# Attention over channels and a gelu MLP on one core: v of block 2 turned on TensorE, the last chunk's steps in order of landing, the first loads in halves

## The chip, the cores and the metric

The kernel runs on 1 core of one Trainium2 chip. The time is what the device takes for one execution, in microseconds (us); runs of the kernel before and of the changed kernel are taken on the same chip and compared. A profiled execution gives the trace: each instruction with its engine, its start and its length, and each DMA with its issue and landing. The engines are TensorE (PE; its weight loads are shown apart as PEld), VectorE (DVE), ScalarE (ACT), GpSimd (POOL) and the sync engine (SP), which here only issues DMAs.

## What is computed

```python
def _attn_ref(q, k, v, tau):                      # q, k, v: 4 x 6080 x 256, tau = 1
    qn = q / (np.linalg.norm(q, axis=1, keepdims=True) + 1e-06)
    kn = k / (np.linalg.norm(k, axis=1, keepdims=True) + 1e-06)
    s = kn.transpose(0, 2, 1) @ qn / tau          # 256 x 256 for each batch
    s = s - s.max(-1, keepdims=True)
    a = np.exp(s)
    a /= a.sum(-1, keepdims=True) + 1e-09
    return (v @ a).astype(np.float32)

def _moe_ref(x, w_in, w_out):                     # x: 24320 x 256
    h = x @ w_in                                  # w_in: 256 x 2048
    c = np.float32(np.sqrt(2.0 / np.pi))
    g = 0.5 * h * (1.0 + np.tanh(c * (h + 0.044715 * h * h * h)))
    return (g @ w_out).astype(np.float32)         # w_out: 2048 x 256
```

The second function is applied to the result of the first. Inputs and output are float32.

## The kernel before

**Stages.** For each batch the kernel needs G = q^T k over all 6080 rows and the sums of squares of the columns of q and k. From these it makes eT, the exponentials of the scaled scores, and then AW = a @ w_in, a 256 x 2048 matrix, so that h = v @ AW needs no separate product with a. For batch 0 this must be done before anything else can start; for batches 1 to 3 it is done a little at a time among the work of the batch before.

**Start (batch 0).** q and k come in six chunks, numbered 0 to 5, of 8, 7, 8, 8, 8 and 8 rows per partition. Chunk 0 is loaded as float32 by two DMAs, q on SP's queue and k on ACT's (`load_first`, L113), and cast on ScalarE (q) and VectorE (k), each in two halves of four rows (`cast_first`, L122 and L124). The other chunks are loaded by POOL with a cast to bf16 on the way (L99); the last one, chunk 5, in five pieces (`PIECES`, `load_last`, L141): q rows 0-3, k rows 0-4, k rows 5-7, q rows 4-5, q rows 6-7. POOL has eight semaphores for its DMAs, so the ninth issue waits until the first has landed, and so on. For each chunk there are squares (q on ScalarE L192/L202, k on VectorE L194/L204), the products G (`gram_row`, L247, two for each row), and the sums of squares as products with ones (`ss_rows`: q by L268, k by L274). `warm(n)` (L369) issues n products whose result nobody reads.

Behind chunk 5 POOL loads the first 512 rows of v (`load_v0(0)`, L314, cast to bf16), w_in in five pieces (L886), half of w_out, v of block 1, the other half of w_out (L647), and v of block 2 by `cast_v`, a cast into DRAM. TensorE runs `warm(8)`, turns v of block 0 (`pe_vt`, L324, eight transposes of 128 x 128 into PSUM), VectorE copies the result into vT (`pe_vt_copy`, L330), and `scores` (L294 to L306) and `first_aw` (L345 to L363) make eT, the row sums, their reciprocals rs and the first columns of AW.

**Blocks.** Then come 48 blocks n = 0 to 47, twelve for each batch, of 512 rows of v (448 in the last of a batch). For each: v transposed into vT (blocks 0 and 1 on TensorE, all others by `cast_v` on POOL, L152, and a transposing DMA on SP, `load_vt`, L162); 2048 columns of h in eight pairs of 256 (`mm1`, L520), except that some sets of two pairs are made by a seven-product scheme (`small`, L596, with sums on VectorE L558 to L561 and L617/L620); gelu on ScalarE (L530, L622, L627, L630) into g; and g @ w_out by the same seven-product scheme on halves (`product`, L725, with seven prepared weights `wcomb`, and sums T1 to T4 on VectorE, L686 to L702). The result is turned on VectorE (L750) and stored by SP (L815).

**The order.** Each engine works through its instructions in program order, and the program order is written out by hand: `WINDOW[n]` names one of the strings in `ORDER` for block n, and its words are issued one after the other, for all engines alike. A word ends in +k or -k when it belongs to block n + k or n - k. The words that matter here: g0 to g7 are pairs of h, G0 to G7 their gelus; awP and acP a part of AW of batch 0 and its copy; T1a, T2a, T2b and so on the sums; M1A to M7B the products with w_out, a half each; p... the preparation of w_out (pA11, pF0, pS1, pF1, pS2, pS4, pS3 on VectorE, L657 to L675; pA12 and pNA on ScalarE, L671 and L673); vs the sums of vT; cq, y5, ap, ax copies and sums of the product's parts; rowI a row of G for the next batch; lq, lk, lv, lt the loads of q, k and v and the transposing load; vtp the turning of v of block 1 on TensorE, vtc0 and vtc1 its copies.

**Buffers.** h uses two buffers of two PSUM banks, so a pair of h waits for the gelu two pairs earlier. Turned v of block 1 uses PSUM tag `s`, as parts of AW do. `load_v0` and the results share the three buffers of the pool `yout`; the two halves of w_out share the two buffers of the squares.

Of the kernel before, what the change touches and what calls it, by code (L numbers as in the profile page):

```python
# [18 lines left out]
def kernel(  # L19
# [10 lines left out]
    nc = tc.nc  # L30
# [75 lines left out]
    def load_first():  # L106


        r0, n = chunks_of(0)[0]
        assert not with_rest(0, 0)  # L110
        st = gp.tile([128, 2, n, 256], FP32, tag="g", name="qk_f32")
        for which, eng in ((0, nc.sync), (1, nc.scalar)):
            eng.dma_start(out=st[:, which], in_=(q, k)[which][0, 0 : R * 128, :].rearrange(  # L113
                "(p r) c -> p r c", r=R)[:, r0 : r0 + n, :])
        return st
# [704 lines left out]
    with tc.manual_schedule():  # L820
# [24 lines left out]
        WARM = [0, 4, 8, 8, 10, 6]  # L845
# [20 lines left out]
        warm(WARM[c])  # L866
        square_rows(c, 0, 0, 4, "act")
        ss_rows(c, 0, range(0, 4))
        square_rows(c, 1, 0, 5, "dve")
        for i in range(4):  # L870
            gram_row(0, c, i)
        ss_rows(c, 1, range(0, 5))
        square_rows(c, 1, 5, 8, "dve")
        square_rows(c, 0, 4, 6, "dve")
        for i in (4, 5):
            gram_row(0, c, i)
        ss_rows(c, 1, range(5, 8))
# [10 lines left out]
        load_v0(1)  # L888
        load_wout(1)
        cast_v(2)  # L890
# [24 lines left out]
        def step(what, n):  # L915
# [28 lines left out]
            elif what[:3] == "vtc":  # L944
                pe_vt_copy(1, int(what[3]))
            elif what[0] == "p":
                prep_wout(what)
            elif what == "lt":
                load_vt(n)
            elif what == "lv":  # L950
                cast_v(n, GATE[0])
            elif what in ("lq", "lk"):
                load_one(b, c, "qk".index(what[1]), GATE[0])
            else:
                mm2_step(n, what)
# [17 lines left out]
    24, 25, 26, 15, 16, 17, 18, 19, 20, 27, 28, 29, 30, 31, 32, 33, 34, 35, 36, 36, 37,  # L973
    38, 39, 40,
]
ORDER = [
    """g0 lt+2 lv+3 aw3 G0 aw2 ac3 g1 ac2 aw5 G1 aw4 lq+1 ac5 g2 SW0 g3 G2 ac4 aw7 G3 aw6 ac7 g4
    ac6 g5 T1a G4 lk+1 vtp G5 g6 vtc0 pA11 g7 G6 vtc1 T2a M1A G7""",
    """g0 pF0-1 lt+2 lv+3 M1B-1 G0 g1 pS1-1 pF1-1 G1 M5A-1 M5B-1 cq-1 g2 pS2-1 lq+1 T2b-1 g3 G2
    pS4-1 M6A-1 G3 M6B-1 g4 pS3-1 y5-1 g5 G4 ap-1 T1a M3A-1 G5 w0m1+1 M3B-1 lk+1 T3b-1 g6  # L980
    pA12-1 vs+1 g7 G6 c12-1 T3a-1 M7B-1 G7 M2B-1 T4a-1 M2A-1 T4b-1 pNA-1 M7A-1 w0m5+1 ax-1""",
    """g0 w0cq T3b-1 lt+2 w0y5 lv+3 row1-1 c11a-2 M4A-2 G0 T2b-1 w0m6 M5B-1 w0ap row3-1 ksq-1
    M4B-2 T2a-1 w0m2 w0m7 row0-1 w0ax w0m3 g3 w0Gq c21-2 lq+1 T3a-1 M5A-1 G3 M1B-1 T4a-1 M1A-1
    c22-2 w0Gx g4 SW1-2 y5-1 cq-1 g5 c11-2 G4 lt+3 lv+4 vs+1 w0m4 M6B-1 w0Gr M6A-1 qsq-1 g6
    ap-1 T1a lk+1 M3A-1 G6 row2-1 M3B-1 f1-1 w0m1+1 G5 M7A-1 T4b-1 w0m5+1 M7B-1 w0y5+1 c12-1
    row5-1 row3 ax-1 w0cq+1 row2 T2a row4-1 g7 ksq f2-1 w0m6+1 row0 w0ap+1 M4B-1 G7 M2A-1
    M2B-1 qsq M4A-1 c11a-1""",
    """g0 f3-2 c21-2 w0m7 G0 w0m2 T2b-1 w0m3 M5A-1 w0ax M1A-1 w0Gq T3a-1 g3 vs+1 w0Gx M1B-1 G3
    w0m4 f1-1 lq+1 M5B-1 g4 cq-1 c22-2 w0Gr w1m5 T1a G4 M6B-1 M6A-1 lt+3 lv+4 w1m1 y5-1 row1-1
    f2-1 w1cq g7 ap-1 w1y5 T4b-1 w1m6 G7 row5-1 w1ap M3A-1 lk+1 row4-1 T3b-1 M3B-1 qsq w0m5+1  # L990
    c12-1 w1m7 w1m2 w1ax w1m3 M7B-1 w1Gq T4a-1 M2A-1 w1m4 c11-2 M2B-1 w1Gr T2a M7A-1 w0y5+1
    row0 ax-1 w0m1+1 w1Gx""",
    """g0 c11a-2 w0cq T3b-1 M4A-2 G0 T3a-1 row5-1 w0m6 M4B-2 f3-2 ksq-1 row2-1 w0ap g3 c21-2
    T2b-1 w0m3 G3 w0m7 w0m2 w0ax M5B-1 lq+1 M1A-1 w0Gq T4a-1 M1B-1 f4-2 w0m4 cq-1 M5A-1 w0Gr
    f1-1 w1m5 M6A-1 y5-1 w1m1 M6B-1 f2-1 w1cq lt+3 lv+4 g4 ap-1 w1y5 c22-2 w0Gx w1m6 c11-2
    M3B-1 w1ap G4 M7B-1 vs+1 row3-1 M3A-1 qsq lk+1 w1m7 f3-1 g7 w1ax T4b-1 w1m3 G7 row4-1 w1m2
    c12-1 w1m4 row1-1 f4-1 M7A-1 w1Gr row2 w1Gq ax-1 M2A-1 T1a w0m1+1 w0m5+1 M2B-1 w0y5+1""",
    """g0 T2a-1 w0cq w1Gx-1 M4A-2 c11a-2 T4a-1 w0m6 G0 M4B-2 w0ap M5A-1 ksq-1 M5B-1 c22-2 c21-2
    row1-1 w0m2 vs+1 w0m7 w0m3 g3 w0Gq w0ax lq+1 T2b-1 M1B-1 G3 w0m4 c11-2 M1A-1 T3a-1 g4 w0Gr
    f1-1 cq-1 w1m5 G4 row4-1 M6A-1 lt+3 lv+4 T4b-1 w1m1 M6B-1 f2-1 y5-1 w1cq g7 ap-1 w1y5  # L1000
    T3b-1 w1m6 G7 M3A-1 w1ap lk+1 M3B-1 M7B-1 w0Gx c12-1 w1m7 ksq M7A-1 w1ax w1m3 w0m5+1 ax-1
    w1m2 w1m4 T1a M2A-1 w1Gr M2B-1 w1Gq row4 c11a-1 row3-1 w0m1+1 f3-1 row0-1 w0cq+1 M4B-1
    c11-1 M4A-1 w0y5+1 row5-1 qsq c21-1 w0m6+1""",
    """g0 w0ap f4-2 M5A-1 w1Gx-1 w0m3 c22-2 w0m7 G0 w0m2 w0ax row2-1 M1A-1 w0Gq T3a-1 M1B-1 w0m4
    T2a-1 g3 cq-1 T3b-1 w0Gr lq+1 M5B-1 G3 f1-1 g4 T2b-1 row0-1 G4 w1m1 M6A-1 T4a-1 w1m5 f2-1
    M6B-1 lt+3 lv+4 y5-1 w1cq g7 ap-1 w1y5 f3-1 w1m6 w0Gx row1-1 w1ap M3B-1 G7 M3A-1 vs+1 lk+1
    w1m7 w1m2 ksq row5-1 w1ax M7B-1 M7A-1 c12-1 T1a w1m3 w1m4 M2A-1 w1Gr M2B-1 ax-1 w1Gq
    w0m5+1 T4b-1 row3-1 w0m1+1 row1 c11a-1 w0cq+1 row0""",
    """g0 T2a-1 w0y5 c11-2 w1Gx-1 w0m6 M4B-2 w0ap G0 M4A-2 f4-2 row4-1 w0m3 qsq-1 w0m7 c22-2 g3
    w0ax w0m2 c21-2 G3 M5A-1 T2b-1 lq+1 w0m4 M1A-1 f1-1 w0Gr row3-1 M1B-1 w0Gq T4a-1 row5-1  # L1010
    w1m1 w1m5 T4b-1 cq-1 M5B-1 w1cq g4 f2-1 lt+3 lv+4 w1y5 T3a-1 w1m6 y5-1 M6A-1 G4 w1ap
    row2-1 M6B-1 f3-1 w0Gx w1m2 T3b-1 w1m3 w1m7 qsq lk+1 g7 ap-1 w1ax M7A-1 f4-1 G7 M3B-1 vs+1
    w1m4 M3A-1 w1Gr M7B-1 c12-1 w1Gq row1 ax-1 w0m5+1 w0m1+1 T1a M2A-1 w0cq+1 M2B-1 w1Gx""",
    """g0 c22-2 w0y5 c11a-2 row2-1 T3a-1 G0 w0m6 M4B-2 w0ap M5B-1 ksq-1 T2b-1 M4A-2 w0m7 c21-2 g3
    w0ax M1A-1 f1-1 G3 w0m2 w0m4 M1B-1 T2a-1 w0Gr w0m3 M5A-1 f2-1 cq-1 T3b-1 row4-1 w0Gq w1m5
    w1m1 c11-2 M6B-1 T4b-1 y5-1 M6A-1 w0Gx lt+3 lv+4 g4 ap-1 w1cq T4a-1 w1y5 M3A-1 f3-1 G4
    w1m6 M3B-1 w1ap row3-1 M7A-1 qsq c12-1 w1m3 vs+1 M7B-1 g7 ax-1 ksq T1a row4 row0 w1m7
    M4A-1 w1ax M2A-1 G7 f4-1 M2B-1 w1m4 c11a-1 row5-1 w1Gr w1m2 f1 M4B-1 w1Gq row1 row2 row0-1
    f2 row5 w0m5+1 f3 w0m1+1 T3a""",
    """lq+4 g0 w0cq c21-2 w0y5 M5B-1 T2a-1 G0 w0m6 M1A-1 w0ap M1B-1 w1Gx-1 f4-1 row3-1 w0m7 cq-1  # L1020
    g3 T2b-1 gc w0ax w0m3 G3 w0m2 M5A-1 T4a-1 w0m4 ss c11-2 w0Gr T3b-1 w0Gq w1m5 sv M6A-1
    T4b-1 pow w1m1 y5-1 M6B-1 c22-2 w1cq g4 lt+3 lv+4 ap-1 w1y5 vs+1 w1m6 G4 M7A-1 w1ap lk+4
    M7B-1 kf M3A-1 w0Gx ax-1 g7 kr T1a w1m7 G7 M3B-1 w1m3 c12-1 w1m2 krp w1ax w1Gq M4A-1 S1+1
    w0m5+1 w1m4 S0+1 w1Gx M2A-1 T2a w1Gr M2B-1 T3a w0y5+1 M4B-1 w0m1+1 th0+1 c21-1""",
# [197 lines left out]
```

## Time and profile before

| | us |
|---|---|
| median of 4 runs | 697.99 (697.83 to 698.2) |
| the profiled execution's own time | 698.2 |
| its span, first to last instruction | 696.4 |
| TensorE busy in the span | 675.4 |
| first product of h | 38.48 |
| TensorE idle before 38.48 | 13.68 |
| TensorE idle from 38.48 to 680 | 0.63 |
| TensorE idle in the last 16.4 us | 6.64 |

The idle times are the lengths of the stretches less TensorE's busy time in them (0.00, 8.89, 7.73 and 8.18 us busy in the stretches from 0, 10, 20 and 30 on). The mean granted clock of TensorE is 0.998. The two loads of chunk 0 landed 8.4 and 8.6 us after their issue at 0.74. A line of the timeline gives start, length, engine, line, operation, tiles and how often; "idle before <-releaser" is how long the engine stood and what ended it.

### The profile page before, as it was taken

How to read it: one execution, taken by the hardware profiler on the slowest of the kernel's cores; microseconds unless marked ns; L12 is line 12 of the kernel's file. 1: busy time of each engine (PE TensorE's matmuls, PEld its weight loads, DVE VectorE, ACT ScalarE, POOL GpSimd, SP SyncE). 2: the span in 40 equal slices, each digit the busy share in tenths (PEclk: the TensorE clock that was granted, in tenths of full speed). 3: DMA queues.
4: the chain of work that ended last, by engine and by line, in shares of the span. 5: the costliest groups of instructions: out<-in, count | busy, mean ns of one | idle time of the engine just before them, and what ended most of it. 6: DMA issues, size and time to landing. Idle time of an engine off the chain costs nothing.

```text
span 696.4 us, 14406 instructions
## 1 busy us (share of the span) xinstructions
PE 675.4 (97%) x5499; PEld 530.5 (76%) x5499; DVE 630.0 (90%) x1243; ACT 616.7 (89%) x894; POOL 73.1 (11%) x135
## 2 busy tenths in 40 slices
PE   3899999999999999999999999999999999999996
PEld 2756778777777777777777777777777888888785
DVE  4489899999998889999999889999999999999996
ACT  5279999998889999998888999999888999999993
POOL 4321100111001001101010010010000000000000
PEclk9999999999999999999999999999999999999999
DMA  9999886775787976747577787683564464453315
GB/s 242 207 262 136 141 150 123 124 107 98 118 129 116 131 128 109 114 81 126 86 131 126 118 126 125 96 138 56 79 101 67 77 103 74 71 99 59 59 34 88
DMA packets 161733, 79.33 MB, mean 114 GB/s; under 512 B 149472, under 2 KB 152672, under 8 KB 160672
## 3 DMA queue, kind: packets, MB, share of 16 engines
q0 software_dynamic: 13952, 39.72, 34.8%
q1 hardware_dynamic: 146608, 37.41, 32.0%
q10 hardware_dynamic: 1104, 1.28, 0.6%
q8 instruction: 43, 0.70, 0.4%
q14 instruction: 26, 0.21, 0.1%
HBM read 78.91 MB, written 36.83 MB: 166 GB/s over the span
## 4 chain that ended last, share of the span: by engine, by line
PE 93%; DMA 4%; DVE 1%; issue 0%; ACT 0%; POOL 0%; DVEq 0%; ACTq 0%; POOLq 0%
PE r L725 23%; PE h L520 22%; PE p L725 17%; PE rb L596 13%; PE qp L596 9%; PE G L247 5%; DMA t<-in_k_dram 2%; PE awp L460 2%; DMA t<-in_q_dram 1%; PE ss L281 0%; DVE xw L620 0%; PE ss L274 0%; PE warm L369 0%; PE rk L405 0%; DVE t L686 0%
## 5 line engine op out<-in xcount | busy, mean ns | idle before, releaser
L725 PEld LDWEIGHTS <-wcomb 128*128 128x128 bf16 x2688 | 262.4, 98 | 42.7 <-issue 0.2
L530 ACT ACTIVATE g<-h 128x1024 bf16<-128x1024 f32 (+1 forms) x178 | 179.7, 1014 | 16.2 <-PE h L520 14.8
L725 PE MATMUL r<-t,wcomb 128*128 128x256 bf16 (+1 forms) x1152 | 164.7, 271 | 0.1
L520 PE MATMUL h<-vT,aw 128*128 128x512 bf16 (+1 forms) x648 | 164.6, 377 | 0.1
L622 ACT ACTIVATE g<-qp 128x1024 bf16<-128x1024 f32 (+1 forms) x103 | 104.6, 1015 | 5.8 <-PE qp L596 3.9
L725 PE MATMUL p<-g,wcomb 128*128 128x256 bf16 (+1 forms) x760 | 106.7, 271 | 0.0
L520 PEld LDWEIGHTS <-aw 128*128 128x128 bf16 x712 | 69.4, 98 | 49.0 <-issue 0.7
L596 PEld LDWEIGHTS <-sw 128*128 128x128 bf16 x824 | 80.2, 98 | 27.5 <-issue 0.9
L192 ACT ACTIVATE sq<-t 128x1536 bf16<-128x1536 bf16 (+4 forms) x59 | 79.3, 1359 | 7.3 <-DMA t<-in_q_dram 7.3
L617 DVE TENSOR_TENSOR qp<-rb,yw 128x512 f32<-128x512 f32 (+1 forms) x103 | 71.0, 689 | 12.7 <-PE rb L596 8.8
L596 PE MATMUL rb<-tv,sw 128*128 128x256 bf16 (+1 forms) x412 | 78.0, 271 | 0.2 <-DVE qp L617 0.2
L620 DVE TENSOR_TENSOR xw<-rb,yw 128x512 f32<-128x512 f32 (+1 forms) x103 | 69.5, 675 | 4.9 <-PE rb L596 4.1
L596 PEld LDWEIGHTS <-aw 128*128 128x128 bf16 x618 | 60.4, 98 | 13.0 <-issue 1.4
L612 ACT ACTIVATE qp<-rb 128x512 f32<-128x512 f32 (+1 forms) x103 | 59.7, 580 | 10.4 <-PE rb L596 5.8
L630 ACT ACTIVATE g<-xw 128x512 bf16<-128x512 f32 (+1 forms) x103 | 63.3, 625 | 1.6 <-DVE xw L620 1.5
L615 ACT ACTIVATE yw<-qp 128x512 f32<-128x512 f32 (+1 forms) x103 | 61.2, 594 | 3.9 <-PE qp L596 2.1
L627 ACT ACTIVATE g<-rb 128x512 bf16<-128x512 f32 (+1 forms) x103 | 61.1, 596 | 3.8 <-PE rb L596 2.6
L698 DVE TENSOR_TENSOR t<-g,t 128x1024 bf16<-128x1024 bf16 (+1 forms) x96 | 63.6, 667 | 0.6
L700 DVE TENSOR_TENSOR t<-g 128x1024 bf16<-128x1024 bf16 (+1 forms) x96 | 63.8, 672 | 0.0
L702 DVE TENSOR_TENSOR t<-t,g 128x1024 bf16<-128x1024 bf16 (+1 forms) x96 | 63.5, 669 | 0.0
L247 PE MATMUL G<-t 128*128 128x256 bf16 (+1 forms) x352 | 58.1, 273 | 1.6 <-DMA t<-in_k_dram 1.6
L686 DVE TENSOR_TENSOR t<-g 128x2048 bf16<-128x2048 bf16 (+1 forms) x48 | 57.4, 1196 | 0.1
(131 smaller groups left out, 879.6 us busy)
## 6 DMA issues: line engine op xcount, KB each, us to landing
out_dram<-ot SPq DMA_DIRECT2D x174, 128.0 KB, 3.0
vb<-in_v_dram POOLq DMA_DIRECT2D x42, 256.0 KB, 4.6
t<-in_q_dram POOLq DMA_DIRECT2D x21, 384.0 KB, 5.1
t<-in_k_dram POOLq DMA_DIRECT2D x21, 384.0 KB, 6.2
wst<-in_moe_w_out_dram POOLq DMA_DIRECT2D x2, 1024.0 KB, 10.4
t<-in_q_dram POOLq DMA_DIRECT2D x3, 512.0 KB, 15.1
t<-in_k_dram POOLq DMA_DIRECT2D x3, 512.0 KB, 17.0
out_dram<-ot SPq DMA_DIRECT2D x12, 112.0 KB, 2.6
```

The lines of the kernel that those rows point to most:

```text
L192: nc.scalar.activation(o, t[:np_, r, :], AF.Square)
L247: nc.tensor.matmul(G[b][:, jc, :], lhsT=qt[:np_, r, jc * 128 : jc * 128 + 128], rhs=kt[:np_, r, :], start=first and jc == 0, stop=jc == 1, ...
L520: mm = nc.tensor.matmul(hp[:, u, :cols], lhsT=AW[b][:, cc, fc * 128 : fc * 128 + 128], rhs=vt_tiles[n][:, cc, :cols], start=cc == 0, stop= ...
L530: nc.scalar.activation(gs(n)[:, 2 * p : 2 * p + 2, :cols], HP.pop((n, p))[:, :, :cols], AF.Gelu_apprx_tanh)
L596: GATE[0] = nc.tensor.matmul(acc[:, u * hc : u * hc + hc], lhsT=lhs[:, u * 128 : u * 128 + 128], rhs=rhs, start=m in (1, 5) and u == 0, st ...
L617: nc.vector.tensor_add(qp(n, i)[:, 1, :c], RB[n, i][:, :c], YW[n, i][:, :c])
L620: nc.vector.tensor_add(XW[n, i][:, :c], RB[n, i][:, :c], YW.pop((n, i))[:, :c])
L622: nc.scalar.activation(gs(n)[:, 2 * pa : 2 * pa + 2, :c].rearrange("p u (t x) -> p t u x", t=2), QP.pop((n, i))[:, :, :c].rearrange("p t ( ...
L698: nc.vector.tensor_sub(o, quarter(n, 1, 1, f0, f1), ts[1][:, f0:f1, :hc])
L700: nc.vector.tensor_sub(o, quarter(n, 1, 1, f0, f1), quarter(n, 0, 1, f0, f1))
L702: nc.vector.tensor_sub(o, ts[2][:, f0:f1, :hc], quarter(n, 1, 0, f0, f1))
L725: nc.tensor.matmul(ACCS[n, acc][:, :hc], lhsT=wcomb[:, w, fc, :], rhs=x, start=first and k == 0, stop=k == 3, skip_group_check=True)
```

## The change

- `load_first` issues four DMAs instead of two: rows 0 to 3 of q on SP and of k on ACT, then rows 4 to 7 on the same queues.
- The six dummy products ahead of chunk 5 are left out. In chunk 5, the sums of squares of q rows 0-3 go behind the first four rows of G, and those of k rows 5-7 ahead of the next two rows of G.
- v of block 2 is loaded by `load_v0(2)`, between v of block 1 and the second half of w_out, instead of `cast_v(2)` behind it. It is turned on TensorE (new word vtq, at the end of block 0) and copied on VectorE (vtr0 and vtr1, at the start of block 1). The transposing load of block 2 (lt+2 in block 0) is gone.
- `ORDER` has new strings for blocks 0 to 16, and `WINDOW` has been renumbered. Apart from the words just named, all words are there as often as before, in another order and partly in another block. From block 17 on the order on TensorE is the same as before; in blocks 18, 21, 25 and 30 loads move by a place or two.

```diff
--- before.py
+++ after.py
@@ -109,9 +109,10 @@
         r0, n = chunks_of(0)[0]
         assert not with_rest(0, 0)
         st = gp.tile([128, 2, n, 256], FP32, tag="g", name="qk_f32")
-        for which, eng in ((0, nc.sync), (1, nc.scalar)):
-            eng.dma_start(out=st[:, which], in_=(q, k)[which][0, 0 : R * 128, :].rearrange(
-                "(p r) c -> p r c", r=R)[:, r0 : r0 + n, :])
+        for h in range(2):
+            for which, eng in ((0, nc.sync), (1, nc.scalar)):
+                eng.dma_start(out=st[:, which, h * 4 : h * 4 + 4], in_=(q, k)[which][0, 0 : R * 128, :].rearrange(
+                    "(p r) c -> p r c", r=R)[:, r0 + h * 4 : r0 + h * 4 + 4, :])
         return st
 
     def cast_first(st):
@@ -842,7 +843,7 @@
         win_bf = const.tile([128, 2, D], BF16)
         wcomb = const.tile([128, 7, 8, 128], BF16)
         nch = len(chunks_of(0))
-        WARM = [0, 4, 8, 8, 10, 6]
+        WARM = [0, 4, 8, 8, 10]
         for c in range(nch - 1):
             if c == 0:
                 cast_first(first)
@@ -863,18 +864,17 @@
         c = nch - 1
         ss_rows(c - 1, 1)
         ss_rows(c - 1, 0)
-        warm(WARM[c])
         square_rows(c, 0, 0, 4, "act")
-        ss_rows(c, 0, range(0, 4))
         square_rows(c, 1, 0, 5, "dve")
         for i in range(4):
             gram_row(0, c, i)
+        ss_rows(c, 0, range(0, 4))
         ss_rows(c, 1, range(0, 5))
         square_rows(c, 1, 5, 8, "dve")
         square_rows(c, 0, 4, 6, "dve")
+        ss_rows(c, 1, range(5, 8))
         for i in (4, 5):
             gram_row(0, c, i)
-        ss_rows(c, 1, range(5, 8))
         ss_rows(c, 0, range(4, 6))
         square_rows(c, 0, 6, 8, "dve")
         for i in (6, 7):
@@ -886,8 +886,8 @@
             nc.gpsimd.dma_start(out=win_bf[:, :, f0:f1], in_=wi[:, :, f0:f1])
         load_wout(0)
         load_v0(1)
+        load_v0(2)
         load_wout(1)
-        cast_v(2)
         warm(8)
         pe_vt(0, "r")
         scores(0)
@@ -943,6 +943,10 @@
                 pe_vt(1, "s")
             elif what[:3] == "vtc":
                 pe_vt_copy(1, int(what[3]))
+            elif what == "vtq":
+                pe_vt(2, "s")
+            elif what[:3] == "vtr":
+                pe_vt_copy(2, int(what[3]))
             elif what[0] == "p":
                 prep_wout(what)
             elif what == "lt":
@@ -970,94 +974,95 @@
 
 WINDOW = [
     0, 1, 2, 3, 4, 5, 6, 7, 8, 9, 10, 11, 12, 13, 14, 15, 16, 17, 18, 19, 20, 21, 22, 23,
-    24, 25, 26, 15, 16, 17, 18, 19, 20, 27, 28, 29, 30, 31, 32, 33, 34, 35, 36, 36, 37,
-    38, 39, 40,
+    24, 25, 26, 27, 28, 17, 18, 19, 20, 29, 30, 31, 32, 33, 34, 35, 36, 37, 38, 38, 39,
+    40, 41, 42,
 ]
 ORDER = [
-    """g0 lt+2 lv+3 aw3 G0 aw2 ac3 g1 ac2 aw5 G1 aw4 lq+1 ac5 g2 SW0 g3 G2 ac4 aw7 G3 aw6 ac7 g4
-    ac6 g5 T1a G4 lk+1 vtp G5 g6 vtc0 pA11 g7 G6 vtc1 T2a M1A G7""",
-    """g0 pF0-1 lt+2 lv+3 M1B-1 G0 g1 pS1-1 pF1-1 G1 M5A-1 M5B-1 cq-1 g2 pS2-1 lq+1 T2b-1 g3 G2
-    pS4-1 M6A-1 G3 M6B-1 g4 pS3-1 y5-1 g5 G4 ap-1 T1a M3A-1 G5 w0m1+1 M3B-1 lk+1 T3b-1 g6
-    pA12-1 vs+1 g7 G6 c12-1 T3a-1 M7B-1 G7 M2B-1 T4a-1 M2A-1 T4b-1 pNA-1 M7A-1 w0m5+1 ax-1""",
...
+    """g0 lv+3 aw3 G0 aw2 g1 ac2 ac3 aw4 G1 aw5 lq+1 ac4 g2 ac5 g3 G2 aw6 G3 g4 ac6 SW0 aw7 G4 g5
+    lk+1 ac7 vtp G5 pA11 g6 vtc0 g7 vtc1 G6 T1a vtq G7""",
+    """g0 vtr0-1 vtr1-1 lt+2 lv+3 g1 T2a-1 G0 T2b-1 M1B-1 G1 pF0-1 g2 g3 G2 pS1-1 w0m1+1 pF1-1
+    lq+1 M1A-1 G3 g4 cq-1 pS2-1 pNA-1 g5 pS4-1 M6B-1 G5 M5A-1 pS3-1 M6A-1 G4 M5B-1 g7 vs+1
+    y5-1 g6 ap-1 G7 T3a-1 lk+1 M3A-1 T3b-1 pA12-1 M7A-1 T4b-1 w0m5+1 M7B-1 w0cq+1 row0 ax-1
+    row1 w0y5+1 M3B-1 T4a-1 G6 w0m6+1 M4B-1 c12-1 w0ap+1 M4A-1 qsq M2A-1 c21-1 M2B-1 row2
+    c11a-1 M1B ksq T1a w0m2+1 w0m7+1 w0m3+1""",
...
```

## The prediction

> **What bounds the kernel now.** I read the page first, then the busy time by stretches, then the chain of waits, then the first 75 us of the timeline with the time that each DMA took to land. The page says that TensorE is nearly all of the chain:
>
> ```profile
> span 696.4 us, 14406 instructions
> ...
> PE 675.4 (97%) x5499; PEld 530.5 (76%) x5499; DVE 630.0 (90%) x1243; ACT 616.7 (89%) x894; POOL 73.1 (11%) x135
> ...
> PE 93%; DMA 4%; DVE 1%; issue 0%; ACT 0%; POOL 0%; DVEq 0%; ACTq 0%; POOLq 0%
> ```
>
> The stretches (columns: stretch, length, busy time and count of each engine, granted clock, DMA share, GB/s) show where TensorE is not full:
>
> ```profile
> 20.00:30.00 10.00, 7.73 (x81) 6.42 (x79) 4.20 (x4) 3.85 (x3) 2.71 (x4) 1.00 1.07 211
> 30.00:38.48 8.48, 8.18 (x105) 6.86 (x103) 4.43 (x11) 3.82 (x9) 5.22 (x7) 1.00 1.29 201
> 38.48:60.00 21.52, 21.52 (x127) 12.04 (x128) 19.95 (x34) 18.04 (x20) 3.31 (x6) 1.00 1.11 232
> 60.00:140.00 80.00, 80.00 (x637) 62.15 (x636) 73.14 (x144) 76.77 (x103) 10.05 (x19) 1.00 0.82 134
> 140.00:200.00 60.00, 59.76 (x474) 45.68 (x473) 57.51 (x118) 53.40 (x83) 7.28 (x12) 1.00 0.68 108
> 200.00:680.00 480.00, 479.61 (x3921) 381.91 (x3919) 451.08 (x899) 446.54 (x666) 34.80 (x65) 1.00 0.61 98
> ```
>
> From 38.48, the first h product, to 680 TensorE idles 0.24 + 0.39 = 0.63 us. So the time is: when h starts, plus the TensorE work behind it, plus those idle tenths, plus a drain that is not touched. Before 38.48 the DMA engines are full (share 1.07) and TensorE is not. The chain of waits tells what sets 38.48 (columns: start, length, what):
>
> ```profile
> 11.28 17.40 DMA t<-in_k_dram
> 28.68 0.04 issue
> 28.72 1.91 PE G L247 x16
> ...
> 31.88 0.68 PE warm L369 x6
> ...
> 35.56 0.90 PE warm L369 x8
> 36.45 0.46 PE vt_ps L324 x8
> 36.91 0.02 issue
> 36.94 0.76 DVE vT_pe L330 x2
> 37.69 0.14 DVE rs L353
> ...
> 37.93 0.50 DVE aw L363
> 38.43 0.05 issue
> 38.48 1.04 PE h L520 x4
> ```
>
> k of chunk 4 lands at 28.68; from there TensorE runs without a gap to 36.91, then VectorE copies the turned v, and h follows. Six warm products lie in that run.
>
> **The change, part by part.** All sums are against the profiled execution: span 696.4, its time 698.2, so 1.8 lie around the span. It was the highest of the four runs; their median, 697.99, is 0.2 lower.
>
> *The warm products and the order of the last chunk.* Six warm products go: 0.68 us out of a run without gaps. The rest of that run keeps its pieces (G, the sums of squares), in another order. Taking the pieces in the new order from 31.88: G 0.90, ss q 0.18, ss k 0.54 and 0.33, G 0.44, ss q 0.08, G 0.46, ss q 0.08, so the end is 34.89 instead of 35.56. The data are there, by issue plus landing time: k rows 0-4 at 15.15 + 16.3 = 31.45 (wanted 31.88), k rows 5-7 at 32.4 (their sums wanted 33.50), q rows 4-5 at 33.1 (wanted 33.83), q rows 6-7 at 20.68 + 13.0 = 33.7 (wanted 34.35), v of block 0 at 23.39 + 11.7 = 35.1 (wanted 35.8). ScalarE's lnk, which waited 3.95 us for the k sums and began at 34.98, now begins near 33.9; so eT is ready near 36.3 and still before VectorE has done its copies (36.26 to 37.0). The copies stay last, and h starts at 37.80: **-0.68**. If eT were late instead, its gain would be the smaller; if a landing is late, the next piece is. The first columns of w_in land at 26.60 + 9.2 = 35.8, wanted 36.4; the next at 28.97 + 7.5 = 36.5, wanted 36.8.
>
> *v of block 2.* Eight turns on TensorE, like those at 36.45, are 0.44 to 0.46 us in a stretch with no idle time: **+0.45**, all on the path. Two copies on VectorE are 2 x 0.42 = 0.84 us; VectorE is busy 19.95 of 21.52 there, and the rest covers them except in block 1 (below). What goes is a cast on POOL (0.54) and one DMA transpose on SP (three take 11.52 us from 48.42); nothing on the chain waited for these, so this gives 0. In POOL's queue the new load of v stands before the second half of w_out, which landed at 36.11 + 11.2 = 47.3. The load of v of block 1 landed 1.1 us behind the first half of w_out (34.58 + 9.8 = 44.4 against 33.68 + 9.6 = 43.3), and v of block 0 1.4 us behind the last q (35.1 against 33.7); so w_out now lands at 48.4 to 48.7. It is first needed by pF0, which I place near 50.3 (37.8 + 12.5, below); cover 1.6 us, after which each us is a us of TensorE.
>
> *The first loads in halves.* The same bytes in 512 instead of 256 packets. Whole packets of 8 KB take 309 ns in the packet records; a halved packet of the converting loads takes 173 against 324, 0.534 and not 0.5. So 256 x 309 x 0.068 / 16 engines = 0.34 us more at most, 0 at least; a gain is excluded, since the engines are full from 2 to 55 us and the bytes stay. Because the chain hangs on the landing at 28.68, this goes whole to the end. I take the middle, **+0.17**. The first half comes some 3 us sooner, so casts (0.69 and 1.05 each) and eight of the sixteen first products move up, and chunk 0 is done 1 to 1.7 us sooner. That is worth 0: it is hidden by the landings of chunks 1 to 4, for which TensorE idles 2.3 of the 10 us from 20 on. If DMA weren't full, it would be worth that 1 us. SP and ACT each issue one DMA more, 0.40 us; behind them ACT has a table load of 1.28 that ends long before 5 us.
>
> [...]
>
> *The new order of blocks 0 to 16.* The instructions are the same, but block 0 now has no products with w_out, VectorE's pF0 moves from 10.3 us after the first h (48.77) to behind T2a and T2b, and pNA moves up between the gelus of block 1. By the rows: TensorE does in block 0 eight pairs of h (0.864 each), six awp (0.432) and two turns (0.45), 10.4 us after the first h. VectorE's T1a ends then too, its two copies near 11.3, T2a and T2b at 12.5, pF0 to pS2 took 52.50 - 48.77 = 3.73, so S2 is there at 16.2; the product M6 that needs it has its turn at 10.4 + six pairs (5.18) + M1 (0.87) + 0.22 = 16.7. Then pS4 and pS3 (55.37 - 53.10 = 2.27), the v sums (58.5 - 57.44 = 1.06) and the add of L775 (0.42) end at 19.95; M3 has its turn at 16.7 + 1.74 + 1.73 = 20.15. It fits by 0.2. With instructions strictly end to end VectorE is 0.6 later: 0 to 0.55 us of stall. Later blocks can lose idle time (0.24 from 140 to 200: -0.23) or gain as much. I take **+0.3** for this part, with ends -0.23 and +0.8.
>
> Sum: -0.68 + 0.45 + 0.17 + 0.3 = +0.24. Span 696.6, and by the median of the runs 697.99 + 0.24, **698.2 us**. With all low ends 697.5, with all high ends 698.0 - 0.68 + 0.46 + 0.34 + 0.8 = 698.9.
>
> **The rivals.**
>
> *Slower: block 1 is too full.* Place: VectorE's weight preparation comes later and ScalarE's copy pNA (L673, 1.06; before at 60.22, behind the gelus of block 1) sooner, while TensorE has few other products to put between the pairs of h. If S2 comes after M6's turn, the products that should hide pNA wait, and the gelus behind pNA and the 0.38 of the copy before it hold the banks that h needs. Price: 0.55 + 1.06 + 0.38 = 1.99 on a sum of -0.06 for the other parts, so 699.9. It decides from the moment that VectorE's copies of the turned v begin more than 0.5 us after block 1's first h. For it: the margin of 0.2 us, and 19.95 busy of 21.52 already. Against: the six pairs, M1 and the 0.22 before M6 keep TensorE busy 6.3 us, in which ScalarE has only 4 gelus, one copy and pNA, 5.5 us.
>
> *Faster: the loads end sooner.* If the halves let chunk 4 land 1.2 us sooner, h starts at 36.6; -1.2 - 0.68 + 0.45 = 696.6. For it: the DMA share of the first 10 us is only 0.84. Against: nothing in the change starts a byte sooner, and from 10 on the share is over 1.
>
> *The gain at the start is not had.* A different end of the chain takes over (w_in's second piece has 0.3 us, eT 0.7): +0.68 on my sum, 698.9. That the halves don't free the first cast, because it waits for both, would cost nothing.
>
> **How the numbers follow.** My forecast has 0.50, the lost gain 0.12, block 1 too full 0.27, loads sooner 0.11. A difference of 0.2% is 1.4 us, about what a measurement can tell from none: the first two, 0.62, lie within it; slower is 0.27, faster 0.11. The range leaves out the faster case and reaches just over the price of the slower one: 697.0 to 700.0; the likeliest case's own is 697.5 to 698.9.
>
> **What would show it.** The chain's landing of chunk 4's k at 28.7 to 29.0; no warm products behind its G; first h at 37.8 to 38.1; 24 turns of v instead of 16; TensorE without idle time from there to 680 but for some tenths. I am wrong if TensorE's idle time behind the first h grows by over 1 us, if block 1 shows ScalarE or VectorE as its releaser, or if the landing at 28.68 moves by more than 0.4.

## The result, and the profile after

The changed kernel takes 696.64 us in the median of 35 runs (696.33 to 696.91) against 697.97 of 53 runs of the kernel before (697.7 to 699.04): ratio 0.9981, 95% interval 0.9976 to 0.9985. So it is faster by 1.33 us, 0.19%, where 698.2 was forecast. The profiled execution's span is 695.1 us for 696.4. The page of the changed kernel, cut to the lines that answer to those of before (its span, busy time by engine, shares of the chain):

```profile
span 695.1 us, 14413 instructions
...
PE 677.2 (97%) x5501; PEld 531.4 (76%) x5501; DVE 630.6 (91%) x1245; ACT 616.2 (89%) x894; POOL 73.3 (11%) x135
...
PE 97%; DMA 1%; DVE 1%; ACT 0%; issue 0%; SPq 0%; DVEq 0%
```

TensorE's share of the chain rose from 93% to 97% and that of DMA fell from 4% to 1%. The busy time by stretches of the changed kernel (columns as before: stretch, length, busy time and count of PE, PEld, DVE, ACT, POOL, granted clock, DMA share, GB/s):

```profile
20.00:30.00 10.00, 10.00 (x108) 8.60 (x108) 4.13 (x4) 3.99 (x3) 2.71 (x4) 1.00 1.07 211
30.00:37.95 7.95, 7.58 (x101) 6.43 (x98) 4.37 (x11) 3.79 (x9) 5.43 (x7) 1.00 1.30 201
37.95:60.00 22.05, 22.05 (x136) 12.58 (x137) 19.24 (x34) 19.01 (x21) 3.35 (x6) 1.00 1.14 230
60.00:140.00 80.00, 80.00 (x638) 62.07 (x636) 74.57 (x147) 74.92 (x100) 10.11 (x19) 1.00 0.81 128
140.00:200.00 60.00, 59.99 (x474) 45.71 (x472) 56.95 (x116) 54.51 (x84) 6.93 (x12) 1.00 0.70 113
200.00:680.00 480.00, 479.80 (x3927) 382.45 (x3925) 452.33 (x900) 445.98 (x666) 34.87 (x65) 1.00 0.61 98
```

The first h stands at 37.95 (38.48 before), and from there to 680 TensorE idles 0.21 us (0.63 before). From 20 to 30 us it idles not at all, where it idled 2.27 us. The chain of waits of the changed kernel says why (columns: start, length, what):

```profile
1.21 9.45 DMA qk_f<-in_q_dram
...
11.78 1.92 ACT sq L193
...
17.10 3.52 PE G L248 x16
...
24.71 0.87 PE warm L370 x8
25.58 1.75 PE G L248 x16
...
27.96 1.09 PE warm L370 x10
29.06 1.75 PE G L248 x16
...
37.95 1.04 PE h L521 x4
```

It no longer goes through the landing of chunk 4's k. It goes from the second half of q of chunk 0, which lands at 10.66, over ScalarE and VectorE to TensorE, which from 17.10 on has no pause; the warm products of chunks 2 to 4 lie in it, which before filled its pauses.

To say where 1.33 us went I set the two traces beside each other, last instruction to last instruction: the start of each ScalarE activation against its twin's in the kernel before, median of 15 around a time. Zero is the kernel before, and negative is earlier:

| part | changed kernel, us | forecast |
|---|---|---|
| first h | -0.53 | -0.51 (-0.68 and +0.17) |
| blocks 0 to 16 (to 320 us) | +0.34 | +0.75 (+0.45 and +0.3) |
| blocks with the same order in both (320 to 680 us) | -0.60 | 0 |
| from there to the end of the span | -0.53 | 0 |
| sum | -1.32 | +0.24 |

The first two rows are what the prediction worked out. The other two, 1.13 of the 1.32 us, are in places where the diff moves at most a load by a place or two. The 0.60 comes in two steps, 0.37 at 331 us and 0.23 at 591. VectorE's timeline at the first, in the kernel before (columns: start, length, engine, line, operation, tiles, count, and in brackets how long it had stood and what ended that):

```profile
329.97 0.65 DVE L698 TENSOR_TENSOR t<-g,t 128x1024 bf16<-128x1024 bf16 x1
331.12 0.69 DVE L620 TENSOR_TENSOR xw<-rb,yw 128x512 f32<-128x512 f32 x1 [0.50 <-PE rb L596]
331.73 0.68 DVE L698 TENSOR_TENSOR t<-g,t 128x1024 bf16<-128x1024 bf16 x1
```

and the same three instructions in the changed kernel:

```profile
329.78 0.65 DVE L699 TENSOR_TENSOR t<-g,t 128x1024 bf16<-128x1024 bf16 x1
330.56 0.69 DVE L621 TENSOR_TENSOR xw<-rb,yw 128x512 f32<-128x512 f32 x1
331.17 0.68 DVE L699 TENSOR_TENSOR t<-g,t 128x1024 bf16<-128x1024 bf16 x1
```

The same subtract waits 0.50 us in the one and not in the other. The releaser named, the product rb, had ended 0.48 us before it began, and the wait itself was over 0.41 us before. TensorE is held up by it. In the kernel before:

```profile
330.70 1.04 PE L725 MATMUL r<-g,wcomb 128*128 128x256 bf16 x8
331.87 0.38 PE L596 MATMUL rb<-tv,aw 128*128 128x256 bf16 x2
```

and in the changed one:

```profile
330.51 1.04 PE L726 MATMUL r<-g,wcomb 128*128 128x256 bf16 x8
331.38 0.38 PE L597 MATMUL rb<-tv,aw 128*128 128x256 bf16 x2
```

From the first of the eight products to the one behind them it is 1.17 us before and 0.87 after. The page counts only 0.13 of these 0.30 us as idle, because by it the eight last 1.04 us, in the changed kernel until 0.17 us behind the start of the next product. So TensorE's idle time from 200 to 680 us fell by only 0.19 us (0.39 to 0.20), while all engines moved ahead by 0.60.

### The profile page after: what moved, and what is told of

Its sections match the earlier page's. It is cut to its first block, busy times and chain, and to the rows that moved or that the text cites. A ratio compares the mean times of both kernels' runs of the same rounds, so it can differ in the third digit from the quotient of the medians.

```text
span 695.1 us, 14413 instructions
## 1 busy us (share of the span) xinstructions
PE 677.2 (97%) x5501; PEld 531.4 (76%) x5501; DVE 630.6 (91%) x1245; ACT 616.2 (89%) x894; POOL 73.3 (11%) x135
## 4 chain that ended last, share of the span: by engine, by line
PE 97%; DMA 1%; DVE 1%; ACT 0%; issue 0%; SPq 0%; DVEq 0%
PE r L726 24%; PE h L521 22%; PE p L726 18%; PE rb L597 13%; PE qp L597 10%; PE G L248 6%; PE awp L461 2%; DMA qk_f<-in_q_dram 1%; PE warm L370 1%; PE ss L275 1%; PE ss L282 0%; ACT sq L193 0%; PE ss L269 0%; PE vt_ps L325 0%; PE rk L406 0%; DVE a L212 0%
## 5 line engine op out<-in xcount | busy, mean ns | idle before, releaser
L521 PE MATMUL h<-vT,aw 128*128 128x512 bf16 (+1 forms) x624 | 158.5, 377 | 0.0
L248 PE MATMUL G<-t 128*128 128x256 bf16 (+1 forms) x352 | 60.0, 279 | 0.0
```

The costliest lines, as they stand in the source:

```text
L248: nc.tensor.matmul(G[b][:, jc, :], lhsT=qt[:np_, r, jc * 128 : jc * 128 + 128], rhs=kt[:np_, r, :], start=first and jc == 0, stop=jc == 1, ...
L521: mm = nc.tensor.matmul(hp[:, u, :cols], lhsT=AW[b][:, cc, fc * 128 : fc * 128 + 128], rhs=vt_tiles[n][:, cc, :cols], start=cc == 0, stop= ...
```

## The experiments

All 18 kernels are timed against the kernel before on the same chip, whose median there was 697.94 to 698.02. The parts are from one profile each, worked out as in the table above. A profiled execution need not be a typical one: that of hw took 698.59 us, 0.79 above its median. And the first h differs by some tenths from execution to execution: it stands at 38.16 to 38.48 in the three traces (before, v_only, dve2) whose start is not edited.

| kernel | median (range), us | ratio, 95% | first h | blocks 0-16 | 320-680 | end |
|---|---|---|---|---|---|---|
| h_only | 697.61 (697.41-698.45) | 0.9997 [0.9989, 1.0006] | -0.19 | 0.00 | -0.02 | -0.47 |
| w_only | 698.23 (697.74-701.76) | 1.0013 [1.0002, 1.0024] | -0.67 | +0.68 | -0.01 | +0.02 |
| hw | 697.80 (696.87-702.29) | 1.0005 [0.9991, 1.0018] | -1.14 | +1.99 | 0.00 | -0.46 |
| v_only | 697.64 (697.42-697.97) | 0.9997 [0.9988, 1.0006] | -0.32 | +0.33 | -0.49 | +0.22 |
| vw | 697.09 (696.74-697.22) | 0.9986 [0.9977, 0.9995] | -0.91 | +0.35 | -0.46 | -0.08 |
| vh | 697.47 (697.07-697.74) | 0.9993 [0.9984, 1.0001] | -0.40 | +0.36 | -0.59 | -0.50 |
| hw_early | 697.96 (697.13-701.8) | 1.0005 [0.9994, 1.0015] | -0.58 | +0.12 | 0.00 | -0.61 |
| hw_turn | 698.58 (698.24-698.9) | 1.0009 [1.0, 1.0018] | -0.73 | +1.05 | +0.04 | -0.32 |
| hw_turn2 | 698.76 (698.13-699.53) | 1.0011 [1.0002, 1.002] | -0.84 | +1.09 | +0.05 | -0.07 |
| hw_order | 704.91 (704.5-705.4) | 1.0097 [1.0083, 1.0111] | -0.67 | +8.29 | -0.44 | -0.51 |
| dve2 | 697.38 (697.21-697.47) | 0.9989 [0.998, 0.9998] | -0.22 | -0.10 | -0.51 | +0.03 |
| after7 | 697.89 (697.59-698.31) | 0.9998 [0.9989, 1.0007] | -0.85 | +0.95 | -0.01 | -0.50 |
| dve2h | 697.29 (696.94-697.66) | 0.9991 [0.9982, 1.0] | +0.15 | -0.09 | -0.51 | -0.14 |
| q_half | 697.77 (697.43-698.14) | 0.9997 [0.9988, 1.0006] | -0.04 | +0.01 | -0.01 | -0.40 |
| k_half | 697.82 (697.66-698.26) | 0.9999 [0.999, 1.0008] | +0.03 | +0.02 | 0.00 | -0.07 |
| fewer | 696.58 (696.29-698.44) | 0.9983 [0.9974, 0.9992] | -0.95 | +0.33 | -0.59 | -0.51 |
| fewer2 | 698.12 (696.37-699.27) | 0.9992 [0.9982, 1.0003] | -0.91 | +0.34 | -0.59 | -0.55 |
| q_fewer | 697.02 (696.71-697.57) | 0.9985 [0.9976, 0.9993] | -0.79 | +0.33 | -0.49 | -0.18 |

### The three edits, alone and together

h_only has the halves alone, w_only the last chunk's new order without its six warm products, hw both, v_only the turning of v of block 2 with the new order of blocks; vw and vh add one edit of the start to that. The edits are the parts of the diff shown above:

```
h_only:  for h in range(2): ... st[:, which, h*4 : h*4+4]
w_only:  WARM = [0, 4, 8, 8, 10]; no warm(WARM[c]) in the last chunk; its ss_rows behind the G rows
v_only:  load_v0(2) for cast_v(2); vtq, vtr; the new ORDER and WINDOW
```

Two theories stand in the expectations of these first four. By S the time follows the first product of h one for one and the rest is as before: for h_only a first h from 0.2 us sooner to 0.3 later than 38.48, and 697.8 to 698.3. By O the gain comes from the new order of the blocks, not from the start.

> The kernel before with only the first loads in halves. [...] Theory O (the gain comes from the new order of the blocks, not from the start): no difference, within 0.3 us of before. [...]

> The kernel before with only the six warm products left out and the sums of chunk 5 in the new order. Theory S: first h at 37.8, time 697.3 (-0.68). Theory O: first h at 37.8 as well, but the 0.7 us is lost again behind it, 697.7 to 698.0.

> Both edits of the start, blocks as before. Theory S: first h near 37.95 as in the changed kernel, time 697.4 to 697.5. Theory O: 697.7 to 698.0, so that most of the 1.33 us is left for the blocks.

> Only v of block 2 turned on TensorE, with the new order of blocks 0 to 16; the start as before. Theory S: the turns cost 0.45 us and the new order gives back 0.1, first h at 38.5, time 698.3. Theory O: the new order takes 1 us or more of idle time out of TensorE behind the first h, so 697.1 to 697.5 in spite of the turns.

> The changed kernel with the first loads whole again. Theory F: first h at 37.5 to 37.9, engines ahead of before's by 0.8 to 1.1 us at 680 us, but the end from there no shorter than before's, as in every kernel without halves: 696.9 to 697.3. Theory O: the sum of the two edits alone, 697.9. If halves give the end its 0.5 us, this kernel's drain shows none of it; if it does, the halves are not the cause.

> The changed kernel with the six warm products and the old order of the last chunk's sums back. First h 38.2 to 38.5. Theory F: engines ahead by 0.3 to 0.6 us at 680, the end 0.5 us shorter than before's: 696.9 to 697.3. Theory O: about the same, 697.3; this run tells whether the shorter end goes with the halves, not F from O.

Neither theory of the first four runs holds. The time does not follow the first h: w_only starts h 0.67 us sooner and gains nothing. The order by itself does not bring the gain either: v_only has 0.31 of the 1.33 us, which its interval does not tell from nothing. The edit of the last chunk costs 0.2 to 0.3 us where v still comes through DRAM (before to w_only, h_only to hw; the second lies within hw's own spread) and gains 0.55 to 0.83 where it is turned on TensorE (v_only to vw, vh to the changed kernel). What eats the gain stands in the waits of hw from 38 to 65 us (columns: engine, tile and line, what it waited for, us in total, times, longest):

```profile
PE rb L597 <- DMA vT<-vb: 1.8, 1, 1.8
...
DVE tv L559 <- DMA vT<-vb: 1.1, 1, 1.1
```

and on TensorE's timeline of w_only:

```profile
56.70 0.38 PE L596 MATMUL rb<-vT,aw 128*128 128x256 bf16 x2 [0.53 <-DMA vT<-vb]
```

In the kernel before this product began at 56.68 with no wait:

```profile
56.68 0.38 PE L596 MATMUL rb<-vT,aw 128*128 128x256 bf16 x2
```

vT of block 2 comes by a cast on POOL into DRAM (issued at 37.0 and landed 11.4 us later) and a transposing load on SP behind it. That load is issued at 48.4 to 48.6 in all three kernels, but the time to its landing differs (before, w_only and hw in this order):

```profile
vT<-vb SPq DMA_TRANSPOSE x1, 6.1
...
vT<-vb SPq DMA_TRANSPOSE x1, 8.1
...
vT<-vb SPq DMA_TRANSPOSE x1, 9.0
```

So in the kernel before vT was there at 54.50, 2.2 us ahead of its use; in w_only it came at 56.66 and in hw at 57.48, and TensorE, which was early, stood still. It lands at 54.3 to 55.3 in the six kernels that have this load and the last chunk in its old order (before, h_only, dve2, dve2h, q_half, k_half). What makes it later in w_only, hw and hw_order (57.80) is open; POOL's next cast of v, issued at 50.20 before, 49.53 in w_only and 49.07 in hw, is a candidate that no run tests.

The column "320-680" is a second clear split: among these six and the changed kernel, -0.46 to -0.60 in the four that have the turning with the new order, 0.00 to -0.02 in the three that have not.

### What the old order has behind the start

Two kernels take vT's landing away from hw, one puts it back into the changed kernel:

```
hw_early:  cast_v(2) ahead of load_wout(0), load_v0(1), load_wout(1)
hw_turn:   load_v0(2); block 0: "... T2a M1A vtq G7"; block 1: "g0 vtr0-1 vtr1-1 pF0-1 ..."
hw_turn2:  block 1: "... y5-1 vtr0-1 vtr1-1 g5 ..." in place of that
hw_order:  after, with cast_v(2), "g0 lt+2 lv+3 ..." in block 0, and no vtq, vtr
```

> Both edits of the start on the kernel before, its own order of blocks and its way of v of block 2 through DRAM kept, but the cast of that v is issued on POOL ahead of the two loads of w_out and of v of block 1 instead of behind them, about 2.9 us sooner (33.3 for 36.1 us in the run with both edits of the start). Theory F (the landing of vT of block 2 is a floor under block 1, which ate the start's gain): the wait of 1.82 us at rb<-vT,aw is gone, the products of all later blocks stand about 1.1 us earlier than before's, as first h does (37.3 to 37.6 for 38.48), and with the shorter end seen wherever the loads are in halves the time is 696.3 to 696.9. Theory O (the gain needs the new order of blocks): 697.8 as with both edits of the start alone, the idle reappearing behind another line of blocks 0 to 2.

> Both edits of the start, and v of block 2 turned on TensorE, but the order of blocks is the kernel before's, with only three steps put in: the eight turns at the end of block 0, the two copies at the head of block 1, and no transposing load of block 2. Theory F: no wait for vT at rb, start's gain of 1.1 us kept less 0.45 us of turns and perhaps 0.2 us at DVE in block 1, with the shorter end 696.7 to 697.3. Theory O: 697.8 to 698.3 (both edits of the start, 697.8, and the turns on top).

> The changed kernel with only the turning taken back: v of block 2 goes through DRAM again (cast on POOL behind the loads of w_out, transposing load at the head of block 0), and the new order of blocks stays. Theory F2 (block 1 of the old order has two deadlines just behind it, the landing of vT of block 2 and the combinations of w_out on DVE; the gain needs both the turning and the new order): the new order reads vT of block 2 at about 52.3 us, and the load cannot land before some 56 us, so rb waits 3 to 5 us and the time is 699.5 to 702. Theory O (the new order by itself brings the gain): 696.2 to 697.2.

> As the run with the turns put into the old order, but the two copies of the turned v stand on DVE behind the combinations of w_out (after the add of block 0's y5) and not ahead of them. Theory F2: the wait of 0.55 us at p<-t,wcomb behind DVE's wcomb is gone, and the engines stand 0.5 to 1.0 us ahead of that run from 60 us on: 697.4 to 698.0, with a narrow spread, since no transposing load is waited for. If the old order is bad for another reason: 698.4 to 698.7 as before.

In the profiled execution of hw_early the wait for vT is gone and the blocks keep 0.46 of the 0.58 us; its time, 697.13, is also the lowest of its eleven. Their median is 697.96, so most of its runs lose the gain in a way that no trace here shows. That the products of w_only and hw waited for vT is shown; that moving the cast forward is a cure is not.

hw_turn and hw_turn2 miss the expected gain: what stands behind the landing of vT is VectorE's preparation of w_out. TensorE's timeline of hw_turn:

```profile
51.48 1.05 PE L726 MATMUL p<-t,wcomb 128*128 128x256 bf16 x8 [0.55 <-DVE wcomb L663]
```

VectorE's timeline of hw_turn2:

```profile
48.88 1.22 DVE L661 TENSOR_TENSOR wf<-wst,wst 128x1024 f32<-128x1024 f32 x1 [0.86 <-DMA wst<-in_moe_w_out_dram]
```

and TensorE's of the same kernel:

```profile
56.63 0.60 PE L726 MATMUL p<-g,wcomb 128*128 128x256 bf16 x4 [0.36 <-DVE p L776]
```

With the copies ahead of the combinations the products of block 0 wait for these; with the copies behind them, VectorE waits until 48.88 us for the second half of w_out, which landed at 47.3 in the kernel before and now stands behind the new load of v, and then the add of y5 is late. The start's gain ends in either case (+1.05 and +1.09 in blocks 0 to 16; 0.3 us more of their medians lies outside the span, which is 2.13 and 2.15 us from the time where the others have about 1.8).

hw_order misses in the other direction, 704.91 for 699.5 to 702: the new order reads vT of block 2 sooner than the old one, and of the 8.29 us lost in blocks 0 to 16 one wait on TensorE's timeline is 5.57:

```profile
57.84 0.59 PE L597 MATMUL rb<-vT,aw 128*128 128x256 bf16 x2 [5.57 <-DMA vT<-vb]
```

So with the start's edits the turning without the new order and the new order without the turning both end above the kernel before. Together they cost +0.33 to +0.36 us in blocks 0 to 16, in each of the seven kernels that have both with the VectorE stream as the change leaves it, whatever the start is: the start's gain goes through.

### The place of VectorE's instructions

The late subtract at 331 us is the same in all kernels that change neither v's turning nor VectorE's instructions. If the instructions of VectorE are numbered in the order of the trace, the first as 0 and its waits on semaphores included, the late subtract is number 703 in the kernel before and 696 in the changed one. Other late ones of the kernel before are 319, 831 and 1343, 128 or a multiple of it away. Two kernels change the numbers and nothing else:

```
dve2:    before, nc.vector.memset(halves, 0.5) three times in place of once
after7:  after,  nc.vector.memset(halves, 0.5) eight times in place of once
```

For dve2 two theories were set against each other. By I the place of an instruction in VectorE's stream makes the late starts at 331 and 591 us, so that both are gone or moved: 697.3 to 697.7. By V they belong to the way of v, and both stay: 697.9 to 698.1.

> The kernel before with two more memsets of a 128x4 constant on DVE at the start, nothing else. [...]

> The changed kernel with seven more memsets of a 128x4 constant on DVE at the start. From block 17 on its DVE instructions then have the same numbers in the stream (waits on semaphores counted) as the kernel before's. Theory I (the instruction whose number leaves 63 by 128 starts 0.40 us late when it stands behind a wait, and costs nothing otherwise): the three such places of the kernel before, numbers 703, 831 and 1343 at about 331, 380 and 591 us, come back; the engines fall behind the changed kernel's by 0.37 us at 340 and 0.6 at 600, and the time is 697.1 to 697.4. If the new order or the way of v keeps them away: 696.5 to 696.8.

dve2 does no useful work more than the kernel before and takes 0.64 us less. The subtract at 331 us is number 705 now; VectorE's timeline of dve2:

```profile
329.66 0.65 DVE L698 TENSOR_TENSOR t<-g,t 128x1024 bf16<-128x1024 bf16 x1
330.44 0.69 DVE L620 TENSOR_TENSOR xw<-rb,yw 128x512 f32<-128x512 f32 x1
```

after7 is the changed kernel with its subtract back at 703. It takes 697.89 us: the gain is gone. VectorE's timeline of after7 at the subtract:

```profile
330.07 0.65 DVE L699 TENSOR_TENSOR t<-g,t 128x1024 bf16<-128x1024 bf16 x1
331.20 0.69 DVE L621 TENSOR_TENSOR xw<-rb,yw 128x512 f32<-128x512 f32 x1 [0.48 <-PE rb L597]
```

and at 591 us, where the add began at 590.21 in the changed kernel with no wait shown:

```profile
590.26 0.68 DVE L703 TENSOR_TENSOR t<-t,g 128x1024 bf16<-128x1024 bf16 x1
591.10 0.43 DVE L776 TENSOR_TENSOR p<-r,y 128x256 f32<-128x256 f32 x1 [0.15 <-PE qp L597]
```

Four instructions of after7 begin 0.39 to 0.41 us after the wait ahead of them ends: numbers 191, 319, 703 and 1343, at 110.67, 167.66, 331.20 and 591.10 us. At these four the engines fall behind the changed kernel's by 0.25, 0.35, 0.36 and 0.23 us, 1.19 in all; its first h, 0.32 sooner, hides part of this in the table. I had expected 0.6, from the steps at 331 and 591 that the kernel before shows, and had not reckoned with the two in blocks that differ between the kernels. Number 831 begins late too, in after7 and in the kernel before, and nothing waits for it. Over all the traces of this study, before and after among them, 22 instructions between 45 and 685 us have such a number (63 over a multiple of 128), stand right behind a wait and find VectorE with nothing left to do: each begins 0.39 to 0.42 us late. The some 1,400 others behind a wait with VectorE run dry begin 0.04 late in the median, 95 of 100 of them within 0.05. Behind 23 more waits at such a number VectorE was still at work when the wait ended; 14 of these begin some 0.40 late by the same measure (number 1343 among them), nine do not. With no wait ahead, most show no delay.

The delay at the count is what the runs show; what makes it, they do not.

### The end of the span

```
dve2h:   before, with dve2's two memsets and the loads in halves
q_half:  before, q in two halves on SP, k whole on ACT
k_half:  before, k in two halves on ACT, q whole on SP
```

> The kernel before with the two memsets and the loads in halves, nothing else: no new order, no turning, the six warm products kept. If the two effects add (0.64 us of the memsets, 0.35 of the halves): 696.9 to 697.1, three quarters of the change's gain. If they don't: 697.3 to 697.6.

> Only q in two halves, on SP's queue; ACT issues its one load of k as before. If the shorter end comes from ACT's instruction stream being one longer (its drain starts 0.37 us after the release in the kernel before and 0.09 in those with halves): no gain at the end, 697.8 to 698.0. If from SP's: the last store lands sooner (1.76 for 2.12 us) and the end is 0.3 to 0.5 us shorter.

> Only k in two halves, on ACT's queue. If the shorter end is ACT's: ACT's drain starts 0.09 us after the release and the end is 0.1 to 0.5 us shorter, 697.5 to 697.8. If it is SP's: 697.8 to 698.0.

The end is 0.40 us shorter with q in halves and 0.07 with k in halves; in the kernel before ScalarE's drain begins 0.37 us after the last release but one, and 0.09 in the changed one. q_half keeps the late drain and has the gain, k_half the reverse. So the drain of ScalarE is not what q in halves changes. Nor do the last stores land sooner, as I had thought: counted from VectorE's last instruction, the last one lands at 3.70 us in the kernel before, 3.66 in the changed one and 3.81 in h_only. (The 2.12 and 1.76 us of the expectation run to the end of the wait on SP that is number 335 below, not to the landing.)

The gain is still not steady: of the 14 kernels with q in halves, the changed one among them, ten end 0.40 to 0.61 us sooner and four 0.07 to 0.32 (hw_turn, hw_turn2, dve2h, q_fewer); the five without lie between -0.08 and +0.22. The count of instructions sorts them. If SP's are numbered in the same way, numbers 79, 207 and 335, again 128 apart, begin at least 0.34 us after the end of the one before in each of the 20 traces; each other number that all traces have, but the first wait of the kernel, begins within 0.07 us in at least one. In the kernel before, 335 is a wait behind the last store's landing, for something already done, and its 0.34 us are added to the end. In the changed kernel 335 is the wait for that landing itself, and the delay is over before the store lands. It is over before the last landing in all ten kernels that end 0.40 us sooner or more, and in dve2h, whose last store landed at 4.13 for 3.70. In the other eight it begins 0.21 to 0.35 us after all that it waits for. ScalarE's late drain belongs here too: it is ScalarE's number 1215, 63 over a multiple of 128, in before, w_only, dve2 and q_half, where it begins 0.29 to 0.31 us after its release; in the other sixteen it has another number and begins 0.02 after.

So what the load of q in halves changes is which instruction has number 335, by one more on SP ahead of it. No run moves only that number. dve2h was expected at 696.9 to 697.1 and took 697.29: its last store landed late. The medians of h_only, q_half and k_half are each within their interval of the kernel before.

### Fewer warm products

```
fewer:    after, WARM = [0, 4, 8, 8, 0]
fewer2:   after, WARM = [0, 4, 8, 0, 0]
q_fewer:  after, WARM = [0, 4, 8, 8, 0], k of the first loads whole
```

> The changed kernel without the ten warm products ahead of chunk 4. There TensorE was busy without a break from 20 to 30 us while k of chunk 4 had landed 0.4 us before it was needed. If those products are on the path: first h 0.3 to 0.5 us sooner than 37.95 and the time 696.1 to 696.4. If landings set the pace after all, or the clock falls for the pause: 696.6 to 697.0.

> The changed kernel without the ten warm products ahead of chunk 4 and without the eight ahead of chunk 3. With the ten left out TensorE already waits 1.6 us for k of chunk 4, which lands at about 28.5 us, so the eight have nothing left to give: first h 37.4 to 37.7 and the time as without the ten, 696.4 to 696.7. If the idle before chunk 3 and 4 lowers the clock, chunk 4's products of 128x256 take longer than 0.12 us each and the time is 696.8 to 697.2.

> The changed kernel with only q in two halves and without the ten warm products ahead of chunk 4. If the shorter end belongs to SP's second load and the start to the warm products: the engines' lead of that kernel with k in halves too, 1.2 us at 680, and an end 0.4 us shorter still: 696.3 to 696.6.

The ten warm products ahead of chunk 4 are on the path, as expected. TensorE's timeline of fewer:

```profile
28.48 1.91 PE L248 MATMUL G<-t 128*128 128x256 bf16 x16 [1.60 <-DMA t<-in_k_dram]
37.53 1.04 PE L521 MATMUL h<-vT_pe,aw 128*128 128x512 bf16 x4 [0.36 <-DVE aw L364]
```

The landing is in the chain again, and h begins 0.42 us sooner than in the changed kernel. The profiled span is 694.7, but the median, 696.58, misses the expected 696.1 to 696.4 and cannot be told from the changed kernel's 696.64, which was taken at another time. With the eight ahead of chunk 3 gone too (fewer2), nothing more is gained, and its times fall into two groups, 696.37 to 696.49 at a mean granted clock of 0.998 to 0.999 and 698.10 to 699.27 at 0.994 to 0.997; the trace is of the first group. Behind their waits of 1.60 and 1.44 us for k the sixteen products of chunk 4 take 1.91 us in both traces, as chunk 3's do ahead of the wait. q_fewer has no k in halves, an end of -0.18 with the late wait on SP, and 697.02 for the expected 696.3 to 696.6. No kernel tried here beats the changed one by more than its interval.

## Why the prediction was wrong

**The first h was right in size, with another reason, and partly by luck.** 37.8 to 38.1 was forecast, 37.95 measured, and single executions differ by some tenths (38.16 to 38.48 in the three traces with an unedited start). The six warm products gave about the 0.68 (w_only: 0.67). The halves' +0.17 is not shown as such, being within these tenths (h_only's first h came 0.19 sooner), and "worth 0: it is hidden by the landings of chunks 1 to 4" failed: the second halves land at about 10.0 and 10.7 us, later than the whole loads (issue at 0.74, landed 8.4 and 8.6 later), and chunk 1's sixteen products take 3.52 us in the chain, which is 0.22 each, where chunk 2's take 1.75, 0.11 each. TensorE was thus late enough to make the warm products part of the path. What makes the first products take twice as long is not shown: the granted-clock column reads 1.00 from 10 to 20 us as from 20 to 30. Chunk 0's sixteen products came in one go before (3.56 us from 10.52 on), with chunk 1's at 2.01 us behind them, and come in two eights, 1.89 us each, with a pause of 2.96 us between after.

**The cost of turning and the order of the blocks was over-sized.** +0.45 and +0.3 were forecast, +0.34 measured to 320 us, and +0.33 to +0.36 with every start. Part of that difference is a late VectorE instruction of the kernel before, number 319 at 168.8 us, which the change moved: in dve2, where it is no longer late, blocks 0 to 16 gain 0.10 (0.14 at that place, less 0.03 at number 191, which is late instead). The rival of a block 1 too full did not come: TensorE is busy 22.05 of 22.05 us there.

**"... nothing on the chain waited for these, so this gives 0"**, said of the cast and the transposing load, failed as reasoning, though the sum came out of it unharmed. With h at 38.48 the load landed 2.2 us ahead of its use. With the last chunk's edit it is used sooner and lands 2.2 to 3.0 us later, and TensorE waits 0.53 (w_only) and 1.82 us (hw) for it, most of the +0.68 and +1.99 of these two. The working added up the gain of the start and the removal of v's detour as if each stood alone; w_only and hw show that the first is nothing without the second, and hw_turn and hw_order that the second needs the new order.

**The step that decided: "Later blocks can lose idle time (0.24 from 140 to 200: -0.23) or gain as much".** The working took the 0.39 us of TensorE's idle time from 200 to 680 as fixed, because the instructions and their order there are the same. They are, but their numbers are not. (The 0.24 us from 140 to 200 did go, to 0.01: number 319 stood there.) Seven instructions fewer on VectorE's stream ahead of block 17, waits counted, moved 0.60 us out of those blocks; after7, which gives the numbers back, brings back 0.59 there and costs 0.60 more in blocks 0 to 16. Nor was 0.39 us a bound, since the page counts less than half of such a stop as idle (0.13 of 0.30 us at 331).

**"A drain that is not touched" failed as well:** -0.53 in the changed kernel. Of this some 0.3 us is the wait that is SP's number 335, which now ends under the landing of the last store, and some 0.1 ScalarE's drain, which is no longer its number 1215 (q_half, which keeps the late drain, has -0.40).

Had these two been nothing, the prediction's own parts as measured, -0.53 and +0.34, would give -0.19 and 697.8, in the range of the likeliest case (697.5 to 698.9). The rival that ends near the measured time, "the loads end sooner", is not what happened: h did not start at 36.6. Nor did the halves make the landing of chunk 4's k late: it is used at 28.48 in fewer, the moment it lands, for 28.7 before.

## What to carry to other kernels

A stretch without idle time may have several deadlines right behind each other: before a gain at the start is counted, look up which landings and which engines' results are used within two microseconds of being there, and whether they move with the start. A difference of a few tenths of a per cent in blocks that were not edited is not yet the edit's doing: add a few empty instructions to one engine's stream, ahead of everything, and see if it moves by as much. Here two memsets gave half of the whole gain and seven took all of it away.

## What was not expected of the hardware

- A VectorE instruction whose number in the stream is 63 over a multiple of 128 begins 0.39 to 0.42 us after the wait ahead of it, for 0.04 otherwise, where VectorE has run dry (22 such in these traces); four such numbers cost 1.19 us in 697 (after7). On SP the numbers 79, 207 and 335 begin at least 0.34 us after the one before, in all 20 traces.
- The profile does not show this as such: it names the last producer as releaser ("0.50 <-PE rb"), though that had ended 0.48 us before.
- The detour of v through DRAM, cast and transposing load, took 17.5 us from the cast's issue at 37.0 to the landing at 54.5 us in the kernel before, and 20.1 and 21.4 us in w_only and hw, while other loads were under way (DMA share 1.19 in those 17.5 us).
- A load in halves brought its first half early (VectorE's cast of k at 5.65 us) and its second half later than the whole had come, 10.07 for 9.18 us by the cast that waits for it.
- The times of one kernel with fewer warm products (fewer2) fall into two groups, their medians 1.8 us apart, at granted clocks of 0.998 to 0.999 and 0.994 to 0.997.
